# Converting float64 weights beside a recurrence: scaled high words moved from PSUM to SBUF, level products on two PSUM buffers

## The chip, the cores and the metric

The kernel runs on one core of one Trainium2 chip. The metric is the device time of one execution in microseconds. A core has five engines that run at the same time and meet only through semaphores: TensorE (PE) for matmuls, VectorE (DVE), ScalarE (ACT) and GpSimd (POOL) for work on elements, and SyncE (SP), which here only issues transfers. SBUF is the working memory of 128 partitions. PSUM is the small memory that TensorE writes its products to.

## What is computed

Two blocks, one after the other. The first is a recurrence over 768 time steps for 4 x 8 heads of width 48; the second is a pair of matrix products with a gate between them, on 3072 rows of width 384 and a hidden width of 2048.

```python
def _attn_ref(r, k, v, w, u):
    ...
    for t in range(S):
        kt, vt, rt, wt = (k[:, :, t], v[:, :, t], r[:, :, t], w[:, :, t])
        cur = np.einsum('bhd,bhe->bhde', u[None] * kt, vt)
        y[:, :, t] = np.einsum('bhd,bhde->bhe', rt, state + cur)
        state = wt[:, :, :, None] * state + np.einsum('bhd,bhe->bhde', kt, vt)
    ...

def _moe_ref(x, w_in, w_out):
    h = x @ w_in
    sp = np.maximum(h, 0.0) + np.log1p(np.exp(-np.abs(h)))
    g = h * erf(sp)
    return (g @ w_out).astype(np.float32)
```

r, k, v, w and u arrive as float32. `w_in` and `w_out` arrive as float64, and the kernel turns them into float32 by arithmetic on their 32-bit words.

## The kernel before

**Steps.** The time axis is cut into 12 steps of one 128-token chunk for two of the four batches (`n_steps`). Steps 0 to 3 and step 4 (`DIRECT`) run `attend`; steps 5 to 11 run `attend_late`. While the attention of step s runs, TensorE also works on the matrix products of earlier steps: `hidden` (line 742, the product with `w_in`) of step s-1, and `project` (line 771, the product with `w_out`) of step s-3. These are generators that are cut into pieces, and a piece is pulled at each of eight places in a step (`place(0)` to `place(7)`). In steps 1 and 2 one piece of `hidden` is pulled at each place. Piece number i of `hidden` reads columns 2i and 2i+1 of `w_in_sb`.

**Levels.** `attend` treats a chunk as a tree. For each level 1 to 6 it takes a PSUM buffer from `products`, writes 32 small products of r and k into it (`level_products`, line 444, 64 records in the profile), multiplies r and k by decays on VectorE (`scale`, line 260), and takes the products out of PSUM into `own` (line 661 for level 1, `copy_predicated` on line 456 for levels 2 to 5, two ScalarE copies on line 463 for level 6). The products of the next level read the r and k that line 260 has just scaled. After the six levels come the transposes of k (line 673), their copy `kT` (line 677), the products for the state (line 530), the new state on VectorE and GpSimd (lines 682, 701 to 706), and the products with the state (line 504), after which `xT`, the input of `hidden`, is copied out of PSUM (lines 511 to 514) and completed by small transfers (line 518).

The decays of the next step (`prepare`, line 312) are made on GpSimd, in products of 512, 256, 128, 64, 32 and 16 elements, between the levels.

**Weight conversion.** `convert` works on 16 blocks of 128 x 768 weights, blocks 0 to 7 for `w_in` and 8 to 15 for `w_out`. Each block takes five steps:

- `load` (line 196, SP) brings the 64-bit words into one of three buffers `words`;
- `scale` runs twice on ScalarE: line 209 multiplies the high words by a power of two into `base`, line 211 the low words into `rest` (two buffers);
- `shift` (line 217, VectorE) shifts the bits of `base` left by three;
- `join` (line 225, VectorE) takes the sign bit from `words`, puts it to the shifted bits and writes the block's place in `w_in_sb` or `w_out_sb`;
- and at the end of `join` GpSimd adds `rest` to that place (line 229). Only then may TensorE read the block.

The table `CONVERT` says by hand at which place of which step each of these is issued: `j` is a shift followed by a join, `h` a shift alone, `o` a join alone, `l` a load, `s` the two scalings. Blocks 0 and 1 are converted in step 0, blocks 2 to 7 in step 1, 8 to 13 in step 2, 14 and 15 in step 3. The order of each engine's instructions is the order of the program.

**PSUM.** Per partition, `y` takes 4 KB, the pool of `hidden` and `project` two buffers of 2 KB, and the two buffers `pp0` and `pp1` of `products` 4 KB each. `base` is the buffer `pp1`. So from the first scaling to the last join the levels use `pp0` alone (the flag `converting`), and `base` has one buffer: line 209 of a block can start only when line 225 of the block before it has read `pp1`. In step 1 the products for the state take `pp1`.

```python
n = 0 if turns["converting"] else turns["next"]
...
base = ps_p.tile([P, 2, NP * C], FP32, name="pp1")[:, :, :DM]
...
nc.scalar.mul(out=base, in_=high.bitcast(FP32), mul=2.0**-112)
...
nc.vector.tensor_scalar(
    out=bits, in0=bits, scalar1=3, scalar2=None, op0=ALU.logical_shift_left
)
...
into = weights[i][0].bitcast(I32)
nc.vector.scalar_tensor_tensor(
    out=into, in0=words[:, :, :, 1], scalar=-(1 << 31), in1=bits,
    op0=ALU.bitwise_and, op1=ALU.bitwise_or,
)
nc.gpsimd.tensor_tensor(out=into, in0=into, in1=rest[:], op=ALU.add)
```

Of the kernel before, what the change touches and what calls it, by code (L numbers as in the profile page):

```python
# [11 lines left out]
FP32 = mybir.dt.float32  # L12
I32 = mybir.dt.int32
U32 = mybir.dt.uint32
AF = mybir.ActivationFunctionType
ALU = mybir.AluOpType

P = 128
EP = 64
HC = 64  # L20
NC = 2
# [39 lines left out]
def kernel(  # L61
# [14 lines left out]
    nc = tc.nc  # L76
    PSUM = bass.MemoryType.PSUM

    n_steps, _, _, JP, C = rkw.shape
    NH, D = v.shape[2:]  # L80
    NP = JP // NJ
    NE = NH // JP
    NB, n_pairs = out.shape[:2]
    _, NT, DM = w_out.shape
# [13 lines left out]
    wide = ctx.enter_context(tc.tile_pool(name="wide", bufs=4))  # L98
    outs = ctx.enter_context(tc.tile_pool(name="outs", bufs=2))
    dram = ctx.enter_context(tc.tile_pool(name="dram", bufs=2, space=bass.MemoryType.DRAM))  # L100
    ps_p = ctx.enter_context(tc.tile_pool(name="ps_p", bufs=1, space=PSUM))
# [21 lines left out]
    w_out_sb = const.tile([P, NT, DM], FP32, name="w_out_sb")  # L123
    y = ps_y.tile([P, NE, NJ, NP // 2, C], FP32, name="y")

    turns = {"next": 0, "converting": False}

    def products(shape, n=None):


        if n is not None:
            return ps_p.tile(shape, FP32, name=f"pp{n}")
        n = 0 if turns["converting"] else turns["next"]
        turns["next"] = 1 - n
        return ps_p.tile(shape, FP32, name=f"pp{n}")

# [30 lines left out]
    def near_log(s):  # L167
        return NEAR_LOG - (s == DIRECT)
# [13 lines left out]
    def convert(weights):  # L182

        held = {}

        def load(i):
            if i >= len(weights):
                return  # L190
            dst, src = weights[i]
            if src.dtype == FP32:
                nc.sync.dma_start(out=dst, in_=src)
                return
            words = wide.tile([P, 2, DM, 2], I32, name="words", bufs=3)
            nc.sync.dma_start(
                out=words[:].rearrange("p i n two -> p i (n two)"), in_=src.bitcast(I32)
            )
            held[i] = [words]

        def scale(i):
            if i in held:
                words = held[i][0]
                low, high = words[:, :, :, 0], words[:, :, :, 1]
                base = ps_p.tile([P, 2, NP * C], FP32, name="pp1")[:, :, :DM]
                rest = wide.tile([P, 2, DM], I32, name="rest", bufs=2)


                nc.scalar.mul(out=base, in_=high.bitcast(FP32), mul=2.0**-112)

                nc.scalar.mul(out=rest[:], in_=low.bitcast(U32), mul=2.0**-29)
                held[i] += [base.bitcast(I32), rest]

        def shift(i):
            if i in held:
                bits = held[i][1]
                nc.vector.tensor_scalar(  # L217
                    out=bits, in0=bits, scalar1=3, scalar2=None, op0=ALU.logical_shift_left
                )

        def join(i):
            if i in held:
                words, bits, rest = held.pop(i)
                into = weights[i][0].bitcast(I32)
                nc.vector.scalar_tensor_tensor(  # L225
                    out=into, in0=words[:, :, :, 1], scalar=-(1 << 31), in1=bits,
                    op0=ALU.bitwise_and, op1=ALU.bitwise_or,
                )
                nc.gpsimd.tensor_tensor(out=into, in0=into, in1=rest[:], op=ALU.add)  # L229

        stages = {"l": load, "s": scale, "h": shift, "o": join}
        done = dict.fromkeys(stages, 0)
        for _ in range(3):
            load(done["l"])
            done["l"] += 1
        while True:
            what = yield
            for stage in {"j": "ho"}.get(what, what):
                stages[stage](done[stage])
                done[stage] += 1  # L240
            if weights[0][1].dtype != FP32:
                turns["converting"] = 0 < done["s"] and done["o"] < len(weights)
                turns["next"] = 0

    def rows(e, n=D):
        return slice(e * EP, e * EP + n)
# [181 lines left out]
    def parts_of(s):  # L428

        c, i = divmod(s, SPC)  # L430
        in_t, vt = loaded[s]
        made, tots, tot = ready[s]
        ends = tot.rearrange("p (n h) -> p n h", h=NC)
        return c, in_t, vt, made, states[i][c % 2], states[i][1 - c % 2], ends
# [183 lines left out]
    def attend(s, xT, place, behind):  # L618

        c, in_t, vt, made, S, S_next, ends = parts_of(s)  # L620
        K = in_t[:, 1]
        RK = in_t[:, 0:2]


        following = prepare(s + 1) if s + 1 < n_steps else iter(())
        own = made if s >= DIRECT else att.tile([P, NH, HC], FP32, name="own")

        def keep_busy(*columns):
            zeros = states[1][0][:].rearrange("p n d -> p (n d)")
            for n in columns if not s else ():  # L630
                nc.tensor.matmul(
                    y[:].rearrange("p e j q t -> p (e j q t)")[:, :n], lhsT=ident[:],
                    rhs=zeros[:, :n], start=True, stop=True, skip_group_check=True,
                )

        def stay_warm(times=1, where=None):
            for _ in range(times):
                ps = where or ps_m.tile([P, NP * C], FP32, name="m")
                nc.tensor.matmul(
                    ps[:], lhsT=ident[:], rhs=ws[s][:, :NP], start=True, stop=True  # L640
                )

        if s == DIRECT:
            next(following)
        for level in range(near_log(s) + 1 if s == DIRECT else 1, LOG + 1):
            rk = made[:] if level == 1 else RK
            pp = products([P, NE, JP, HC])
            level_products(pp, rk, level)
            if level == LOG and s == DIRECT:
                spread_blocks(s + 1, pp)  # L650
            scale(s, level)
            keep_busy(DM, DM // 2)
            if level == 1 and s == 1:
                stay_warm()
            if s == 1 and level == 2:
                behind(None)
            got = pp[:].rearrange("p e n t -> p (e n) t")
            if level == 1:
                if not s:
                    nc.vector.tensor_copy(out=first[:], in_=mask_sb[:, 0, :])  # L660
                nc.vector.tensor_mul(
                    own[:], got, first[:, None, :].to_broadcast([P, NH, HC])
                )
            else:
                take_level(own, pp, level)
            if level > 1 and (s, level) != (DIRECT, LOG - 1):
                next(following, None)
            place(level - 1)

        from_own(s, own, 1)  # L670
        ps = products([P, JP, P])
        for n in range(JP):
            nc.tensor.transpose(ps[:, n, :], K[:, n, :], ident[:])  # L673
        if not s:
            stay_warm()
        kT = att.tile([P, NH, D], FP32, name="kT", bufs=1)
        nc.scalar.copy(
            kT[:].rearrange("p (e n) d -> p e n d", e=NE),
            ps[:].rearrange("p n (e d) -> p e n d", e=NE)[..., :D],
        )  # L680
        if c:
            nc.gpsimd.tensor_mul(
                faded[0][:], S[:], ends[:, :, 0:1].to_broadcast([P, JP, D])
            )
        next(following, None)
        place(LOG)


        if s:

            ps = products([P, NC, JP, HC], 1 if s == 1 else None)
            ps = [ps[:, h] for h in range(NC)]
        else:
            ps = [ps_m.tile([P, JP, HC], FP32, name="m") for h in range(NC)]
        state_part(s, kT, ps)
        from_own(s, own, 0)
        if not s:
            stay_warm(1, products([P, NP * C]))
        for e in range(NE):
            if c:  # L700
                nc.vector.tensor_add(middle[rows(e)], faded[0][rows(e)], ps[0][rows(e), :, :D])
            else:
                nc.vector.tensor_copy(middle[rows(e)], ps[0][rows(e), :, :D])
        nc.gpsimd.tensor_mul(faded[1][:], middle[:], ends[:, :, 1:2].to_broadcast([P, JP, D]))
        for e in range(NE):
            nc.vector.tensor_add(S_next[rows(e)], faded[1][rows(e)], ps[1][rows(e), :, :D])
        for _ in following:
            pass
        place(LOG + 1)
        through_state(s, xT)  # L710
        behind()
# [135 lines left out]
    with tc.manual_schedule(  # L847
# [20 lines left out]
        for s in range(n_steps):  # L868
# [34 lines left out]
            def behind(n=0):  # L903
                if n is not None:
                    convert_at(LOG + 2)
                    return
                for what in BEHIND_SCALING:
                    conversion.send(what)
# [6 lines left out]
        s = n_steps - 1  # L915
# [105 lines left out]
```

## Time and profile before

| | |
|---|---|
| time, median of 3 runs | 616.99 us (616.94 to 617.49) |
| span of the profiled execution, first to last instruction | 614.9 us |
| granted TensorE clock | 1.000 |
| matrix products, line 742 / line 771 | 257.3 / 252.1 us |
| conversion on ScalarE: line 209 / line 211, 16 each | 0.888 / 0.912 us each (medians) |
| conversion on VectorE: line 217 / line 225, 16 each | 0.966 / 0.95 us each (medians) |
| conversion on GpSimd: line 229, 16 | 1.81 us at the least, up to 2.72 us |
| conversion, from the first to the last instruction | 25.6 to 120.0 us |

The profile gives no time of its own for the profiled execution beside its span; the median of the timed runs is 2.1 us longer than the span. Times in the profile count from the first instruction. "PEld" is the weight load of TensorE, which runs beside its products. A bracket at the end of a line of the timeline says how long the engine had been idle before the instruction and what released it.

### The profile page before, as it was taken

What the parts mean: (1) busy time and instruction counts of PE and PEld (TensorE: products, weight loads), DVE (VectorE), ACT (ScalarE), POOL (GpSimd) and SP (SyncE); (2) the same over time, 40 slices, a digit from 0 to 9 for tenths busy, and PEclk for the clock granted to TensorE, in tenths of its full rate; (3) what the DMA queues carried; (4) which work ended last, traced back from release to release, by engine and by line L of the source; (5) the groups of instructions that cost most, each with busy time, mean ns of one, the idle gap of its engine ahead of it and who ended that gap; (6) DMA issues with size and microseconds to landing.
All of it is one profiled execution on the core that took longest, in us unless ns stands there. A gap on an engine that the chain in (4) does not pass through costs nothing.

```text
span 614.9 us, 15592 instructions
## 1 busy us (share of the span) xinstructions
PE 602.1 (98%) x6858; PEld 445.9 (73%) x6858; DVE 409.3 (67%) x459; ACT 293.9 (48%) x374; POOL 293.3 (48%) x295
## 2 busy tenths in 40 slices
PE   7889999999999999999999999999999999999997
PEld 6668787678668668668668768768768768668654
DVE  5687696995995897897797797797797311110300
ACT  2548888544446724534534534534534444624600
POOL 4348184603497399299199299299296000000000
PEclk9999999999999999999999999999999999999999
DMA  8376471440353316307307306405303100000000
GB/s 325 117 281 203 184 258 58 164 149 8 136 157 78 101 34 190 112 29 206 101 30 197 109 31 181 126 31 156 117 28 79 25 26 0 9 26 1 0 27 26
DMA packets 51371, 63.27 MB, mean 103 GB/s; under 512 B 34920, under 2 KB 40296, under 8 KB 49896
## 3 DMA queue, kind: packets, MB, share of 16 engines
q1 hardware_dynamic: 50152, 61.68, 31.5%
q8 instruction: 54, 0.88, 0.6%
q10 hardware_dynamic: 1152, 0.59, 0.4%
q14 instruction: 13, 0.11, 0.1%
HBM read 52.39 MB, written 8.69 MB: 99 GB/s over the span
## 4 chain that ended last, share of the span: by engine, by line
PE 85%; DVE 6%; DMA 3%; POOL 2%; issue 2%; ACT 1%; SPq 0%; POOLq 0%; ACTq 0%; DVEq 0%
PE m L771 38%; PE m L742 37%; PE pp L444 4%; DMA w<-in_rkw 3%; PE y L478 2%; PE y L504 1%; PE pp L530 1%; DVE in L260 1%; POOL w_in_sb L229 1%; DVE w_in_sb L225 1%; POOL tot_sb L312 1%; PE pp L673 1%; DVE sums L364 1%; DVE pp L217 1%; DVE own L456 1%
## 5 line engine op out<-in xcount | busy, mean ns | idle before, releaser
L742 PE MATMUL m<-xT,w_in_sb 128*128 128x256 f32 x1152 | 257.3, 382 | 2.4 <-DVE w_in_sb L225 1.2
L771 PE MATMUL m<-w_out_sb,h 128*128 128x384 f32 x768 | 252.1, 488 | 0.0
L742 PEld LDWEIGHTS m<-xT,w_in_sb 128*128 128x128 f32 x1152 | 216.1, 190 | 34.8 <-issue 3.6
L771 PEld LDWEIGHTS m<-w_out_sb,h 128*128 128x128 f32 x768 | 144.6, 190 | 98.5
L751 ACT COPY h<-m 128x512 f32<-128x512 f32 x96 | 56.1, 584 | 130.5 <-PE m L742 130.4
L731 DVE TENSOR_TENSOR h<-h,sp 128x1024 f32<-128x1024 f32 x48 | 74.6, 1594 | 52.1 <-ACT sp L727 51.9
L260 DVE TENSOR_TENSOR in<-in,tot_sb 128x1024 f32<-128x1024 f32 (+1 forms) x60 | 84.4, 1414 | 30.6 <-PE pp L444 27.3
L378 POOL TENSOR_TENSOR words<-words,rest 128x528 f32<-128x528 f32 (+10 forms) x77 | 85.7, 1113 | 6.0
L374 POOL TENSOR_TENSOR rk<-words 128x528 f32<-128x528 f32 (+3 forms) x28 | 44.5, 1588 | 81.2 <-DVE sums L364 70.8
L780 ACT COPY o<-m 128x384 f32<-128x384 f32 x24 | 11.5, 480 | 110.3 <-PE m L771 110.3
L312 POOL TENSOR_TENSOR tot_sb<-tot_sb 128x256 f32<-128x256 f32 (+4 forms) x60 | 54.6, 911 | 4.5
L727 ACT ACTIVATE sp<-sp 128x2048 f32<-128x2048 f32 x24 | 45.9, 1911 | 0.3
L724 ACT ACTIVATE sp<-h 128x2048 f32<-128x2048 f32 x24 | 45.9, 1911 | 0.3
L444 PEld LDWEIGHTS pp<-in 48*64 48x64 f32 (+1 forms) x2368 | 33.8, 125 | 16.3 <-issue 8.5
L364 DVE TENSOR_REDUCE sums<-words 128x6 f32<-128x288 f32 (+8 forms) x66 | 29.2, 470 | 19.4 <-POOL words L374 19.2
L444 PE MATMUL pp<-in 48*64 48x64 f32 (+1 forms) x2368 | 38.3, 212 | 3.7 <-issue 1.6
L727 ACT ACT_TABLE_LOAD x24 | 30.8, 1283 | 15.9 <-issue 13.0
L374 POOL TENSOR_TENSOR words<-words 128x336 f32<-128x336 f32 (+6 forms) x49 | 35.1, 716 | 3.8
L364 DVE TENSOR_REDUCE sums<-rk 128x14 f32<-128x672 f32 (+9 forms) x54 | 34.8, 704 | 0.2
L724 ACT ACT_TABLE_LOAD x24 | 30.8, 1283 | 4.9 <-issue 4.5
L378 DVE TENSOR_TENSOR words<-words,rest 128x576 f32<-128x576 f32 (+8 forms) x34 | 27.9, 820 | 1.2
L229 POOL TENSOR_TENSOR w_out_sb<-w_out_sb,rest 128x768 int32<-128x768 int32 x8 | 17.8, 2222 | 17.8 <-DVE w_out_sb L225 17.7
(80 smaller groups left out, 438.0 us busy)
## 6 DMA issues: line engine op xcount, KB each, us to landing
in<-in_rkw SPq DMA_DIRECT2D x11, 1024.0 KB, 5.6
words<-in_moe_w_in SPq DMA_DIRECT2D x8, 768.0 KB, 4.5
words<-in_moe_w_out SPq DMA_DIRECT2D x8, 768.0 KB, 4.3
words<-in_rk_rows SPq DMA_DIRECT2D x8, 768.0 KB, 6.8
w<-in_rkw SPq DMA_DIRECT2D x11, 512.0 KB, 8.4
v<-in_v SPq DMA_DIRECT2D x12, 384.0 KB, 6.9
out<-o SPq DMA_DIRECT2D x24, 192.0 KB, 1.9
rest<-in_w_rows SPq DMA_DIRECT2D x8, 384.0 KB, 7.3
```

Of the source, the lines that this page charges most:

```text
L260: nc.vector.tensor_mul(halves, halves, view(tots[level - 1], 0, [[1, n], [2, nb], [0, half]]))
L312: nc.gpsimd.tensor_mul(new, pair[:, :, 0], pair[:, :, 1])
L364: nc.vector.tensor_reduce(out=view(sums[:], n, [[near * (NEAR + 1), NEAR // near], [NEAR + 1, near - n]]), in_=terms[n], axis=mybir.AxisLi ...
L374: engine.tensor_mul(terms[n], r[:, :, n:], k[:, :, : near - n])
L378: engine.tensor_mul(k[:, :, :m], k[:, :, :m], w[:, :, n : n + m])
L444: nc.tensor.matmul(pp[s0 : s0 + m, e, n, :m], lhsT=rk[rows(e), 1, n, s0 : s0 + m], rhs=rk[rows(e), 0, n, t0 : t0 + m], start=True, stop=True,)
L724: nc.scalar.activation(held[0][:], h[:], AF.Softplus)
L727: nc.scalar.activation(held[0][:], held[0][:], AF.Erf)
L731: nc.vector.tensor_mul(h[:, part], h[:, part], held[0][:, part])
L742: nc.tensor.matmul(ps[:, ff, :], lhsT=w_in_sb[:, g * FG + f + ff, kk * P : (kk + 1) * P], rhs=xT[:, kk, :], start=kk == 0, stop=kk == KT - 1,)
L751: nc.scalar.copy(h[:, f : f + FT, :], ps[:])
L771: nc.tensor.matmul(ps[j][:], lhsT=gs[g][:, f, j * C : (j + 1) * C], rhs=w_out_sb[:, g * FG + f, :], start=g + f == 0, stop=g == NG - 1 and ...
```

## The change

Three things change. `base` becomes a tile in SBUF with two buffers, and the shift writes its result straight into the block's place in `w_in_sb` or `w_out_sb`, so that the join reads it from there and works in place. With `pp1` free, `products` alternates between `pp0` and `pp1` throughout, and the flag `converting` and the fixed choice in step 1 go. The new tile takes 2 x 3 KB per partition of SBUF, and the program is built with `dynamic_dma_scratch_size=1024` in place of the default.

```diff
-    turns = {"next": 0, "converting": False}
+    turns = {"next": 0}
...
-        n = 0 if turns["converting"] else turns["next"]
+        n = turns["next"]
...
-                base = ps_p.tile([P, 2, NP * C], FP32, name="pp1")[:, :, :DM]
+                base = wide.tile([P, 2, DM], FP32, name="base", bufs=2)
...
-                nc.scalar.mul(out=base, in_=high.bitcast(FP32), mul=2.0**-112)
+                nc.scalar.mul(out=base[:], in_=high.bitcast(FP32), mul=2.0**-112)
...
-                held[i] += [base.bitcast(I32), rest]
+                held[i] += [base[:].bitcast(I32), rest]
...
-                    out=bits, in0=bits, scalar1=3, scalar2=None, op0=ALU.logical_shift_left
+                    out=weights[i][0].bitcast(I32), in0=bits, scalar1=3, scalar2=None, op0=ALU.logical_shift_left
...
-                words, bits, rest = held.pop(i)
+                words, _, rest = held.pop(i)
                 into = weights[i][0].bitcast(I32)
                 nc.vector.scalar_tensor_tensor(
-                    out=into, in0=words[:, :, :, 1], scalar=-(1 << 31), in1=bits,
+                    out=into, in0=words[:, :, :, 1], scalar=-(1 << 31), in1=into,
...
-            if weights[0][1].dtype != FP32:
-                turns["converting"] = 0 < done["s"] and done["o"] < len(weights)
-                turns["next"] = 0
...
-            ps = products([P, NC, JP, HC], 1 if s == 1 else None)
+            ps = products([P, NC, JP, HC])
...
-    nc = bacc.Bacc("TRN2", target_bir_lowering=False, num_devices=1)
+    nc = bacc.Bacc("TRN2", target_bir_lowering=False, num_devices=1, dynamic_dma_scratch_size=1024)
```

## The prediction

> **What bounds the kernel now.** First the busy times of the engines, then busy times by stretch, to see where TensorE is not full.
>
> ```profile
> PE 602.1 (98%) x6858; PEld 445.9 (73%) x6858; DVE 409.3 (67%) x459; ACT 293.9 (48%) x374; POOL 293.3 (48%) x295
> ```
>
> ```profile
> 34.00:58.00 24.00, 22.52 (x404) 17.96 (x408) 21.87 (x24) 15.83 (x25) 16.89 (x12) 1.00 0.79 273
> ```
>
> The columns of the second are the stretch, its length, the busy time of PE, PEld, DVE, ACT and POOL with their instructions, the clock and the transfers. TensorE is the bound; after 120 us nothing of the conversion runs. Whatever the change brings or costs is idle time of TensorE in steps 0 to 3, and it stays to the end, because afterwards TensorE runs almost without a gap (from 127 us on it is busy for 483.2 of 487.9). But from 34 to 58 us (step 1) VectorE is busy for 21.87 of 24 us, nearly as full as TensorE: a level costs TensorE 1.09 us on line 444 and 2.79 us on line 742, together 3.88, and VectorE 3.6 to 3.8 (from one line 260 to the next). Next the timeline of the conversion.
>
> ```profile
> 42.52 1.16 PE L444 MATMUL pp<-in 48*64 48x64 f32 x64 [0.78 <-DVE own L456]
> ...
> 47.76 1.22 DVE L260 TENSOR_TENSOR in<-in,tot_sb 128x1024 f32<-128x1024 f32 x1
> ...
> 47.98 2.67 POOL L229 TENSOR_TENSOR w_in_sb<-w_in_sb,rest 128x768 int32<-128x768 int32 x1 [0.94 <-DVE w_in_sb L225]
> ...
> 49.50 0.97 DVE L217 TENSOR_SCALAR pp<-pp 128x768 int32<-128x768 int32 x1
> ...
> 50.50 0.95 DVE L225 SCALAR_TENSOR_TENSOR w_in_sb<-words,pp 128x768 int32<-128x768 int32 x1
> 50.62 1.04 POOL L312 TENSOR_TENSOR tot_sb<-w 128x512 f32<-128x512 f32 x1
> ...
> 55.04 2.46 PEld L742 LDWEIGHTS m<-xT,w_in_sb 128*128 128x128 f32 x12 [0.24 <-POOL w_in_sb L229]
> ```
>
> Line 444 waited 0.78 us at 42.52 for line 456 to empty the only buffer (0.17 more at 76.12): all that two buffers can return. At 55.04 line 742 waited for GpSimd's line 229, so piece i of `hidden` starts as soon as block i is converted: the conversion is itself on the edge of the critical path. And the shift at 49.50 ran at its full rate in the middle of line 229 (47.98 to 50.65). Its operands are in PSUM. Other instructions of VectorE don't get past GpSimd so easily:
>
> ```profile
> 9.90 1.26 POOL L312 TENSOR_TENSOR tot_sb<-tot_sb 128x128 f32<-128x128 f32 x1
> 10.83 0.39 DVE L660 CAST first<-mask_sb 128x64 f32<-128x64 int32 x1
> ...
> 71.80 1.83 POOL L229 TENSOR_TENSOR w_out_sb<-w_out_sb,rest 128x768 int32<-128x768 int32 x1 [6.71 <-DVE w_out_sb L225]
> 73.23 1.49 DVE L260 TENSOR_TENSOR in<-in,tot_sb 128x1024 f32<-128x1024 f32 x1 [1.57 <-PE pp L444]
> ...
> 117.56 2.41 POOL L229 TENSOR_TENSOR w_out_sb<-w_out_sb,rest 128x768 int32<-128x768 int32 x1
> 118.34 2.25 DVE L378 TENSOR_TENSOR words<-words,rest 128x576 f32<-128x576 f32 x1
> ```
>
> Line 378 needs 0.75 us for this shape and took 2.25, line 260 needs 1.22 and took 1.49: each ended as if it had begun 0.14 us before the recorded end of line 229. The other way, the 2.67 of line 229 at 47.98 is 1.83 after line 260 let go, 0.14 before its end at 48.98. I use this rule everywhere: who comes second waits for the whole instruction of the other, then runs its full time; of two, the one that waits already goes next. (One case breaks the second half: at 111.08 a line 312 stood back for two of line 731.)
>
> [...] the shift from PSUM passed, and the cast at 10.83 (one input, SBUF to SBUF) ended 0.19 us after the GpSimd instruction let go at 11.02. [...] line 285, 256 elements, 0.289 us[...]. [...] here 0.888 us (line 209) against 0.912 (line 211).
>
> **The change, part by part.**
> *Scaling (line 209) to SBUF.* 16 times 0.024 us on ScalarE: nothing, hidden beside VectorE. Its waits for line 225 (10.5 us in all) go, but in steps 1 and 2 VectorE, not ScalarE, comes last. What is late next on ScalarE is line 211, which needs line 229 of two blocks before; by the times below its data are there before the join wants them.
> *Shift (line 217) in SBUF.* Lines 281 and 285 put the fixed part at 0.155 us and the double rate at 0.52 ns per element: 0.155 + 768 x 0.52 = 0.555 us in place of 0.966 (estimate). Bounds: 0.966 if no double rate. [...]
> *Join (line 225).* Same 0.95 us, but its second input is now in SBUF[...].
> *Two buffers for the levels.* The 0.78 and 0.17 us.
> *The build option.* No transfer is issued on GpSimd's queue: nothing.
>
> Step 1 by the rule. VectorE starts 0.09 us before the end of an independent predecessor, 0.03 after one that it needs; GpSimd 0.14 after VectorE; TensorE 0.05 after its releaser. Until 41.1 all stays (`xT` at 34.55 sets TensorE). Line 229 of block 2 runs 41.25 to 43.08. TensorE now starts level 3 at 41.74, but piece 2 needs block 2: 43.13, before 43.61, gain 0.48. Shift 3, ready at 42.28, waits until 42.94 and ends 43.50; join 3 ends 44.48, line 260 45.61 (each 0.26 late); line 229 of block 3, behind line 260, ends 47.30, piece 3 starts 47.35 (gain 0.14). Shift 4, ready 46.15, waits for that until 47.16, ends 47.72 (before 46.85); join 48.70; line 260 49.83; block 4 at 51.52, piece 4 at 51.57 (before 51.37). Shift 5, ready 50.37, waits until 51.38, ends 51.94. Now line 312 (512 elements, 1.04) has waited and goes first, to 52.84; join 5 52.70 to 53.65; line 312 (256, 0.62) to 54.13; line 260 53.99 to 55.21 (before 52.74), block 5 at 56.90 and piece 5 at 56.95 (before 55.04): 1.91 late. Again: shift 6 ends 57.32, join 6 58.39 behind a line 312, line 260 59.62, shift 7 60.14. There join 7 and line 229 of block 6 come within 0.01 us of each other; block 6 is ready at 62.81 or 62.01, so piece 6 starts 3.51 or 2.71 late (before 59.35). Then ScalarE, no longer held by its softplus (it ended at 65.32, line 504 at 65.50), returns 0.16: 3.35 or 2.55; I take 2.95.
>
> Step 2, in the old times. `w_out` isn't needed yet, so only line 260 can stop TensorE. Level 3 starts 0.17 earlier. Shift 10 waits to 80.51, shift 11 to 84.73, join 11 behind line 312 to 86.44, line 260 of level 5 to 88.00: level 6 at 88.05 (before 87.75). Line 260 of level 6 ends 92.41 (before 90.03), the transposes start 0.64 late. Then joins, line 229 twice, line 731 twice and line 682 take turns: line 682 ends at 100.15 (before 97.13), line 701 at 101.30, line 504 starts at 101.35 in place of 100.02: 1.33 late. Behind it stands TensorE's whole queue. Step 3: block 15 is ready at 120.1, before line 771 wants it at 121.08; nothing.
>
> Sum: 2.95 + 1.33 = 4.3 us on the span of 614.9, so 619.2; the median lies 2.1 above the span, and that part stays: 616.99 + 4.3 = 621.3.
>
> **The rivals.** *No double rate*: the shift keeps 0.97 us and passes GpSimd, only the joins meet it. By the same walk join 5 and line 312 meet at 50.6, piece 5 starts 0.74 late and piece 6 1.0 late, of which ScalarE returns 0.15 and step 2 0.17: +0.7, 617.7. For it: no tensor_scalar from SBUF is in the trace. Against: the cast and the copy. *No meeting* (not slower): in steps 1 and 2, shift and join get through beside line 229 although their operands are in SBUF. Then 0.48 + 0.17 us are gained: 616.3. It decides if a shift beside line 229 takes no more than 0.6 us. Against it stand the three cases above. *The same, and the gap of 1.00 us at 67.93* (TensorE waits for `xT`) closes as well: 1.65, 615.3. Against: that gap hangs on the softplus and the transfer of `xT`, which the change doesn't touch. *Worse turns*: [...] step 2 loses as much as step 1, 2 us more: 623.3.
>
> **How the numbers follow.** Main case 0.74 with its own range 619.5 to 623 (one turn of 0.8 us won or lost, the shift 0.1 us off); worse turns 0.05; no double rate 0.08; no meeting 0.06; with the gap 0.07. A measurement can tell 0.2% (1.2 us) from no change. Slower is 0.74 + 0.05 = 0.79, the same 0.08 + 0.06 = 0.14, faster 0.07. The range leaves out the last three, 0.21, and reaches from 618.4 (a third of the cost, if most turns fall as at 111.08) to 624.0 (worse turns, and 0.7 for one more).
>
> **What would show it.** Line 217 at 0.55 us where GpSimd is idle (block 0, at 26.5) and 1.2 to 1.7 us where line 229 runs (blocks 3 to 6); some joins above 0.95; the level 5 instance of line 260 in step 1 ending 2 to 3 us later; line 742 waiting 1 to 2.5 us for line 229 at pieces 5 and 6; no wait of line 444 for line 456. Wrong would be: shifts of 0.55 us in the midst of line 229, or 0.97 everywhere.

## The result, and the profile after

The changed kernel takes 622.62 us (median of 4 runs, 622.08 to 624.16) beside 617.24 us for the kernel before (4 runs, 616.94 to 617.64): a ratio of 1.0090, 95% interval 1.0074 to 1.0106. It is slower, by 5.4 us. The profiled run took 622.43 us, with a span of 620.6 (before 614.9). From line 241 on the lines of the changed kernel carry numbers lower by three: 257 is the old 260, 309 the old 312, 441 the old 444, 739 the old 742, 501 the old 504, 768 the old 771. Below, "the multiply" is line 260/257, "the add" is GpSimd's line 229.

The busy times of the engines on the page, and the same stretch of step 1 as was shown of before (stretch, its length, PE, PEld, DVE, ACT, POOL, clock, transfers):

```profile
PE 602.8 (97%) x6858; PEld 445.7 (72%) x6858; DVE 415.2 (67%) x459; ACT 293.6 (47%) x374; POOL 298.3 (48%) x295
```

```profile
34.00:58.00 24.00, 21.04 (x386) 16.71 (x387) 22.13 (x20) 14.96 (x24) 16.37 (x9) 1.00 0.73 254
```

TensorE has the same work (602.8 us beside 602.1) and 5.7 us more span, so 5 us more idle. VectorE was to be relieved: a shift costs 0.41 us less in SBUF. Yet it is busy for 5.9 us more in all, and in step 1 for 22.13 us in place of 21.87. In the records the time in which an instruction is held up counts as busy: the shift that takes 0.55 us with GpSimd idle is recorded for up to 1.60 us in the timeline of the changed kernel:

```profile
41.94 1.32 DVE L217 TENSOR_SCALAR w_in_sb<-base 128x768 int32<-128x768 int32 x1
...
45.91 1.58 DVE L217 TENSOR_SCALAR w_in_sb<-base 128x768 int32<-128x768 int32 x1
...
48.62 2.69 POOL L229 TENSOR_TENSOR w_in_sb<-w_in_sb,rest 128x768 int32<-128x768 int32 x1 [1.56 <-DVE w_in_sb L225]
...
50.14 1.60 DVE L217 TENSOR_SCALAR w_in_sb<-base 128x768 int32<-128x768 int32 x1
51.27 1.36 POOL L309 TENSOR_TENSOR tot_sb<-w 128x512 f32<-128x512 f32 x1
...
51.77 1.68 DVE L225 SCALAR_TENSOR_TENSOR w_in_sb<-words,w_in_sb 128x768 int32<-128x768 int32 x1
...
53.37 1.63 DVE L257 TENSOR_TENSOR in<-in,tot_sb 128x1024 f32<-128x1024 f32 x1
53.88 2.79 POOL L229 TENSOR_TENSOR w_in_sb<-w_in_sb,rest 128x768 int32<-128x768 int32 x1
...
56.72 2.86 PE L739 MATMUL m<-xT,w_in_sb 128*128 128x256 f32 x12 [0.91 <-POOL w_in_sb L229]
...
59.94 4.39 POOL L229 TENSOR_TENSOR w_in_sb<-w_in_sb,rest 128x768 int32<-128x768 int32 x2
...
62.62 0.70 PE L739 MATMUL m<-xT,w_in_sb 128*128 128x256 f32 x2 [1.42 <-POOL w_in_sb L229]
```

Read it downwards. The add of block 4 starts at 48.62. The shift at 50.14, which in PSUM ran beside it in 0.97 us, now ends at 51.74, 0.43 us after the recorded end of the add. GpSimd's line 309 comes next, the join behind the shift waits for that one (1.68 in place of 0.95), the multiply waits for the next (1.63 in place of 1.23), and the add of block 5, recorded from 53.88, waits in its turn (2.79 in place of 1.81). Piece 5 of `hidden` starts at 56.72 in place of 55.04, piece 6 at 62.62 in place of 59.35. The opening says that the engines meet only through semaphores; here VectorE and GpSimd hold each other up without one, too. The profile's summary of waits has no entry in which VectorE waits for line 229, though the shift at 50.14 took 1.05 us longer than with GpSimd idle. All the shifts of the changed kernel, shortest, median and longest, in ns:

```profile
L217 DVE TENSOR_SCALAR w_in_sb<-base x8: 559/1124/1599, 26.4 to 59.3; 128x768 int32<-128x768 int32 x8
L217 DVE TENSOR_SCALAR w_out_sb<-base x8: 550/778/1575, 73.0 to 118.1; 128x768 int32<-128x768 int32 x8
```

With GpSimd idle a shift takes 0.55 us; beside the add up to 1.6. The summary of waits has TensorE on the add itself (first the kernel before, then the changed one, two lines):

```profile
PEld m L742 <- POOL w_in_sb L229: 0.2, 1, 0.2
```

```profile
PEld m L739 <- POOL w_in_sb L229: 4.0, 5, 1.7
...
PE m L739 <- POOL w_in_sb L229: 3.2, 5, 1.4
```

The columns are us in total, times and the longest. Lastly a piece of the difference that has nothing to do with this waiting. At 440.6 us, long after the conversion, TensorE stops among the 64 small matmuls of line 501 (32 with the state `s`, then 32 with `middle`):

```profile
440.05 0.51 PE L501 MATMUL y<-in,s 48*48 48x64 f32 x23
441.74 0.36 PE L501 MATMUL y<-in,s 48*48 48x64 f32 x9 [1.18 <-issue]
```

"issue" says that nothing which the profile shows was late. In the kernel before, the same list runs through (30 of the 32 records with `s` stand in one row, and the next row follows without a gap):

```profile
435.44 0.86 PE L504 MATMUL y<-in,s 48*48 48x64 f32 x30
```

### The profile page after: what moved, and what is told of

The parts are those of the page before. It is cut to its first block, busy times and chain, and to the rows that moved or that the text cites. A ratio compares the mean times of both kernels' runs of the same rounds, so it can differ in the third digit from the quotient of the medians.

```text
span 620.6 us, 15584 instructions
## 1 busy us (share of the span) xinstructions
PE 602.8 (97%) x6858; PEld 445.7 (72%) x6858; DVE 415.2 (67%) x459; ACT 293.6 (47%) x374; POOL 298.3 (48%) x295
## 4 chain that ended last, share of the span: by engine, by line
PE 82%; DVE 7%; POOL 5%; issue 2%; DMA 1%; ACT 1%; SPq 0%; DVEq 0%; POOLq 0%; ACTq 0%
PE m L768 38%; PE m L739 35%; PE pp L441 4%; DVE in L257 2%; POOL tot_sb L309 2%; PE y L475 2%; PE y L501 2%; POOL w_out_sb L229 1%; PE pp L527 1%; POOL w_in_sb L229 1%; DMA in<-in_rkw 1%; DVE own L453 1%; DMA xT<-y 1%; DVE sums L361 1%; DVE words L375 1%
## 5 line engine op out<-in xcount | busy, mean ns | idle before, releaser
L728 DVE TENSOR_TENSOR h<-h,sp 128x1024 f32<-128x1024 f32 x48 | 77.0, 1644 | 51.6 <-ACT sp L724 51.4
L229 POOL TENSOR_TENSOR w_out_sb<-w_out_sb,rest 128x768 int32<-128x768 int32 x8 | 19.1, 2394 | 17.0 <-DVE w_out_sb L225 13.1
L375 DVE TENSOR_TENSOR words<-words,rest 128x576 f32<-128x576 f32 (+8 forms) x34 | 26.4, 776 | 1.2
```

The lines of the kernel that those rows point to most:

```text
L375: engine.tensor_mul(k[:, :, :m], k[:, :, :m], w[:, :, n : n + m])
L728: nc.vector.tensor_mul(h[:, part], h[:, part], held[0][:, part])
```

## Experiments

Theory: shift and join now have both sides in SBUF, they and GpSimd's instructions wait for each other, and this waiting costs more than the shift gains; the second buffer helps. The late gap comes from the number of TensorE's instructions ahead of it. Rivals: the shift's speed or the join alone is the cost; the second buffer makes it; the late gap is a late effect of the conversion.

The table takes each run's trace apart at one place. *To step 2* is the time from the first product of `hidden` in step 1 to the first product of `project` in step 2 (67.11 us before); *rest* is from there to the end of TensorE's last product (509.83 us before). Both are differences to before; the first holds the conversion, the second almost none of it.

| run | median us | ratio to before (95%) | to step 2 | rest |
|---|---|---|---|---|
| the change | 622.62 | 1.0090 (1.0074–1.0106) | +4.61 | +1.35 |
| e1, change without the add | 616.78 | 0.9992 (0.9982–1.0002) | −1.45 | +1.67 |
| e2, before without the add | 618.80 | 1.0025 (1.0017–1.0033) | +0.28 | +1.57 |
| e3, change, shift at single rate | 620.01 | 1.0042 (1.0028–1.0057) | +1.44 | +1.61 |
| e4, before, join in SBUF | 621.51 | 1.0071 (1.0051–1.0091) | +4.44 | +0.39 |
| e5, change, 22 warm-up multiplies | 621.53 | 1.0063 (1.0046–1.0081) | +4.61 | +0.50 |
| e6, before, 18 warm-up multiplies | 618.28 | 1.0008 (0.9999–1.0016) | −0.02 | +1.60 |
| e7, change with one buffer | 626.34 | 1.0131 (1.0107–1.0154) | +6.98 | +2.83 |
| e8, e4 with 22 warm-up multiplies | 621.79 | 1.0063 (1.0041–1.0086) | +3.14 | +0.24 |
| e9, change, add in halves | 623.50 | 1.0088 (1.0065–1.0112) | +4.28 | +1.97 |
| e10, before, add in halves | 617.90 | 0.9999 (0.9988–1.0011) | +0.49 | +0.20 |
| e11, e3 with the add in halves | 620.43 | 1.0037 (1.0025–1.0049) | +2.04 | +1.69 |

The kernel before had medians of 617.24, 617.40, 617.65 and 617.62 us in the four groups (change; e1 to e4; e5 to e8; e9 to e11). In *rest* two classes stand apart: 0.2 to 0.5, and 1.35 and more. Those of the second all have a gap of 1.1 to 1.5 us in the list of line 504/501 near 436 to 446 us, those of the first don't. What is left, 0.2 to 0.5 us, is mostly another gap in such a list, at 250 to 259 us, which was 0.94 us in the one profiled run of before and 1.0 to 1.4 in the others.

### Without the add (e1, e2)

```diff
-                nc.gpsimd.tensor_tensor(out=into, in0=into, in1=rest[:], op=ALU.add)
```

Both leave out the addition of the low words to the weights.

> The changed kernel without line 229: the low words of the weights are not added, all else stays. GpSimd then has only the decays (line 309) between the levels. Theory [...]: shifts fall to 0.56 us except where line 309 runs, TensorE waits for nothing of the conversion, and the kernel becomes faster than the one before, about 616.0 us (5.4 lost are back, and 0.78 + 0.17 + 0.24 us of waits of the kernel before are gone too). Rival (the cost is in the work on SBUF itself, or in the two buffers for the levels): line 229 was only running beside it, so about 621 to 622.6 us.

> The kernel before without line 229, as the counterpart of the run without it after the change: the low words are not added. Both theories: shifts and joins read PSUM and met nobody, so only 0.24 us (piece 5 waited for line 229) and a part of 0.17 us come back: about 616.9 us. If it fell by a microsecond or more, line 229 would cost something in itself, and the other run could not be read as it stands.

The change without its add costs nothing: 616.78 us, and to step 2 it is 1.45 us faster than before and 6.06 faster than the full change. It lies 0.8 us above the 616.0 expected; its profile has the late gap, with 1.12 us. The shifts of this kernel, where block 5 and 6 are converted:

```profile
49.30 0.55 DVE L217 TENSOR_SCALAR w_in_sb<-base 128x768 int32<-128x768 int32 x1
...
52.51 0.55 DVE L217 TENSOR_SCALAR w_in_sb<-base 128x768 int32<-128x768 int32 x1
53.08 0.96 DVE L225 SCALAR_TENSOR_TENSOR w_in_sb<-words,w_in_sb 128x768 int32<-128x768 int32 x1
```

1.60 us have become 0.55. So it is the meeting with the add, not the new shift or join as such. Taking the add away also takes away TensorE's wait for it, so e1 alone doesn't say how much is this waiting; e2 is there for that. e2 was a miss in size: 618.80 where 616.9 was expected, above before, though an instruction less was asked of GpSimd per block. Most of it, 1.57 us, lies in the rest, with a late gap of 1.19. The 0.28 us up to step 2 come from a meeting that the add had kept away: GpSimd, free early, now begins line 311 (the old 312) just ahead of the multiply.

```profile
44.36 1.04 POOL L311 TENSOR_TENSOR tot_sb<-w 128x512 f32<-128x512 f32 x1 [12.80 <-DMA w<-in_rkw]
44.43 2.04 DVE L259 TENSOR_TENSOR in<-in,tot_sb 128x1024 f32<-128x1024 f32 x1
```

The multiply waits for 0.8 us and TensorE for 0.48 after it. So without the add the two conversions differ by 0.28 + 1.45 = 1.73 us to step 2, in favour of the changed one; with it by 4.61 against it. The meetings with the add have turned the sign.

### The shift at single rate (e3)

```diff
-                base = wide.tile([P, 2, DM], FP32, name="base", bufs=2)
+                base = wide.tile([P, 3, 264], FP32, name="base", bufs=2)[:, :, :256]
```

The rows are kept apart by 8 words, with the scaling's and the shift's views cut to match. With this gap all 16 shifts took 0.93 to 1.00 us, beside GpSimd or not, so the double rate is off; why a gap does that is not shown by a run here.

> The changed kernel with the scaled high words in rows of 256 that have a gap of 8 words between them, 3 rows to a block[...]; the rest is the same. Theory: the shift then [...] takes 0.97 us everywhere, also beside line 229, and only the joins still meet GpSimd: 617.7 us (the rival 'no double rate' of the prediction), so a shift that is slower by 0.4 us makes the kernel 5 us faster. Rival (the joins carry the cost): still 621 us or more, and joins of 1.7 us. If the shift still takes 0.56 us where GpSimd is idle, the gap did not do what it should.

The profile of e3 around the add of block 4 (there line 234; the shift is 221, the join 230, the multiply 262):

```profile
50.05 2.67 POOL L234 TENSOR_TENSOR w_in_sb<-w_in_sb,rest 128x768 int32<-128x768 int32 x1 [0.96 <-DVE w_in_sb L230]
...
51.57 0.93 DVE L221 TENSOR_SCALAR w_in_sb<-base 128x768 int32<-128x768 int32 x1
52.53 1.00 DVE L230 SCALAR_TENSOR_TENSOR w_in_sb<-words,w_in_sb 128x768 int32<-128x768 int32 x1
52.69 1.75 POOL L314 TENSOR_TENSOR tot_sb<-w 128x512 f32<-128x512 f32 x1
...
53.46 2.06 DVE L262 TENSOR_TENSOR in<-in,tot_sb 128x1024 f32<-128x1024 f32 x1
```

The slower shift, SBUF to SBUF as in the change, runs through in the middle of the add in 0.93 us, and the kernel is 2.6 us faster than the change for it: of the 4.61 us up to step 2, 1.44 are left. So it is not the place of the operands alone that makes the shift wait: the one that takes 0.55 us with GpSimd idle needed 1.60 beside the add, the one of 0.93 us did not wait. Joins and multiplies still meet GpSimd (the multiply at 53.46 took 2.06 us in place of 1.21, the join at 57.02 1.56 in place of 1.00), and these 1.44 us, with the 1.61 of the rest (a late gap of 1.44 in it), give 620.01 in place of the 617.7 expected.

### The join in SBUF alone (e4, e8)

```diff
-                    out=bits, in0=bits, scalar1=3, scalar2=None, op0=ALU.logical_shift_left
+                    out=weights[i][0].bitcast(I32), in0=bits, scalar1=3, scalar2=None, op0=ALU.logical_shift_left
...
-                    out=into, in0=words[:, :, :, 1], scalar=-(1 << 31), in1=bits,
+                    out=into, in0=words[:, :, :, 1], scalar=-(1 << 31), in1=into,
```

`base` and the shift's input stay in PSUM. e8 differs from e4 in its warm-up multiplies alone (as e5 below).

> The kernel before, with one part of the change: the shift still reads PSUM, but writes into the weights' place, and the join reads it from there (two inputs in SBUF). Base stays in PSUM, the levels stay on one buffer. Theory: shifts stay at 0.97 us and pass line 229; the join meets line 312 once in step 1, piece 5 starts 0.74 and piece 6 1.0 us later, 0.15 come back: about 618.1 us. Rival (the joins carry the cost): 621 us or more.

> The kernel before with the shift's output in the weights' place (the shift still reads PSUM), as in the run of that before, and with 22 warm-up multiplies instead of 20 (4 of them narrow). That run had a TensorE gap of 1.16 us at 51.3 us in which nothing visible was late, and it came out at 621.5. If that gap depends on the program's layout, it is gone or elsewhere here, and the join's part alone is seen: 618.1 to 619.5 us. If the gap belongs to the edit: 621.5.

Both were dearer than expected. e4 had a second gap of the layout's kind, in the small matmuls of level 5; in e8, four TensorE records further on, it is gone:

```profile
50.20 1.14 PE L444 MATMUL pp<-in 48*64 48x64 f32 x58
...
52.50 0.34 PE L444 MATMUL pp<-in 48*64 48x64 f32 x6 [1.16 <-issue]
```

```profile
50.45 1.16 PE L444 MATMUL pp<-in 48*64 48x64 f32 x64
```

Of 4.44 us to step 2, 3.14 remained. Of these some 1.2 arise up to line 504 of step 2, from joins that wait for GpSimd, as expected. The other 1.9 us had not been thought of; the profile of e8 shows them at the end of step 2:

```profile
102.70 1.12 DVE L706 TENSOR_TENSOR s<-faded,pp 48x384 f32<-48x384 f32 x2 [1.01 <-POOL faded L704]
...
103.96 1.16 PE L444 MATMUL pp<-rk 48*64 48x64 f32 x64 [1.57 <-DVE s L706]
```

The level products of step 3 want the buffer that still holds the products for the state, and their reader, line 706, hangs on GpSimd (lines 682 and 704), which is behind with its adds. In the kernel before, line 706 had ended at 100.43, just ahead of line 444 at 100.57: the wait was 0.14 us from appearing. The medians of e4 and e8 don't differ, because three of e4's and four of e8's six runs had a mean granted clock of 0.997 or less, and took 621.55 to 623.86 and 621.40 to 623.44 us; of the runs above that, e4's are at 620.23, 620.25 and 621.47 us, e8's at 619.81 and 620.32.

### One buffer for the levels (e7)

```diff
-        n = turns["next"]
+        n = 0 if turns["converting"] else turns["next"]
```

with the flag `converting` set as before.

> The changed kernel with the level products on one PSUM buffer while the conversion runs, as in the kernel before; the scaled words stay in SBUF. This takes the change's second half away alone. If the second buffer brings next to nothing, because the level's multiply on VectorE rather than the buffer is what each level waits for: 622.6 us, within 0.5 either way. If it hides a cost of the first half (each level's matmuls then have to wait for the multiply of the level before, which now meets GpSimd): 624 or more.

626.34 us, and 2.37 us more than the change up to step 2. Not all of that is the buffer: in this profile the granted clock was 0.50 from 107.29 to 110.71 us, and the list of small products just before the first product of `project` falls into it.

```profile
106.86 1.67 PE L444 MATMUL pp<-rk 48*64 48x64 f32 x64 [1.57 <-DVE s L706]
```

From the start of this list to that product it is 1.61 us here and 1.10 in e8 at full clock. So 0.51 of the 2.37 us belong to the clock, and the second buffer is worth about 1.9 us up to step 2. Most of this is the wait of 1.57 us for line 706, which the change doesn't have. Another 1.1 us of the clock lies in the first 16 product records of line 771 (6.52 us in place of 5.43), in the rest. The two runs without such a drop, at 624.84 and 624.88, are 2.2 us above the median of the change and 2.4 above its profiled run. So the change's first half alone costs about 6.5 us up to step 2, and its second half takes 1.9 of them back.

### The late gap (e5, e6)

```diff
-        for _ in range(20):
-            nc.tensor.matmul(warm[:], lhsT=ident[:], rhs=ident[:], start=True, stop=True)
+        for n in [P] * 18 + [16] * 4:
+            nc.tensor.matmul(warm[:, :n], lhsT=ident[:], rhs=ident[:, :n], start=True, stop=True)
```

This is e5; e6 is the kernel before with `range(18)`.

> The changed kernel, with 22 warm-up multiplies instead of 20 at its start (18 of full width and 4 of 16 columns, so that they take no more time). The weight conversion is untouched. If the TensorE gap of 1.18 us at 440.6 us, which the kernel before does not have, depends only on how many TensorE instructions stand ahead of that place, it moves off the dense small matmuls and is gone: 621.4 us, 1.2 under the changed kernel, with the conversion's cost of 4.7 us unchanged. If the gap is an effect of the conversion, or of something else that comes late for it, it stays: 622.6.

> The kernel before, with 18 warm-up multiplies instead of 20, and nothing else changed. If the late gap depends only on the number of TensorE instructions ahead of it, this kernel now gets one of about 1.2 us near 437 us: 618.5 us. If the gap comes from the changed conversion, none appears here: 617.3.

The list of line 501 in e5, and of line 504 in e6:

```profile
440.88 0.82 PE L501 MATMUL y<-in,s 48*48 48x64 f32 x30
```

```profile
435.93 0.52 PE L504 MATMUL y<-in,s 48*48 48x64 f32 x24
437.69 0.33 PE L504 MATMUL y<-in,s 48*48 48x64 f32 x8 [1.25 <-issue]
```

Two multiplies more at the start and the gap of the change is gone, with the conversion's cost the same to the hundredth (+4.61); two fewer and the kernel before has it. It belongs to the position in TensorE's program, not to the conversion.

The traces show this position exactly. Number all of TensorE's records (weight loads, products and waits for semaphores) in the order of their starts: in each of the eight traces that have it, the late gap comes after 11,457 records. In all thirteen traces that place falls into this list. Where 21 to 27 of the list's products were out by then, TensorE stops for 1.1 to 1.5 us; where it was 14 to 20, the next product comes within 0.2 us. The change moves the list because its TensorE program has six waits fewer (88 for 94), which is as many records as three products with their weight loads: 23 products are out where it was 20. e2 has eight waits fewer, and has the gap as well. So the gap came with the edit, but through the length of the program and not through the waiting between VectorE and GpSimd.

In the timed runs the steps are blurred: 1.1 us less in e5 than in the change, 0.6 more in e6 than before (interval −0.1 to +1.0).

### The add in halves (e9, e10, e11)

```diff
-                nc.gpsimd.tensor_tensor(out=into, in0=into, in1=rest[:], op=ALU.add)
+                for f in range(2):
+                    nc.gpsimd.tensor_tensor(out=into[:, f], in0=into[:, f], in1=rest[:, f], op=ALU.add)
```

> The changed kernel with GpSimd's add of each block (1.81 us alone) as two instructions of half the block, about 0.9 us each. If whoever comes second waits for one whole instruction of the other, VectorE's shift, join and multiply wait for a half at most: where the shifts of blocks 4 to 6 lasted 1.55 to 1.60 us, at most 1.2 (0.56 of its own and one half, less 0.14), and pieces 5 and 6 come sooner; worked out from the 3.5 us lost there, about half comes back: 621.0 us. Rival: the two keep taking turns, so that each half now waits for one VectorE instruction and the add of a block ends later than before (over 2.8 us for the two): 622.6 or above. A TensorE gap of about 1.2 us in line 501's list may come or go with the layout.

> The kernel before with the same edit. Here only the level's multiply and the add meet (the shift and the join have a PSUM side), so a half as much wait is worth little: 617.0 us, within 0.5 apart from a late gap of about 1.2 us that the layout may bring. Rival: the add's second half comes behind a multiply and the weights come later: 618 or above without such a gap.

> The changed kernel with the shift at single rate (which passes GpSimd) and the add in halves: only joins and multiplies meet the add, and for a half at most. The single-rate shift alone came out at 620.0, with a late gap of the layout in it. If waits go by whole instructions, some 0.8 us of the 1.4 lost there up to step 2's first projection come back: 619.2 us, or 618.0 where the layout brings no late gap. Rival: turns take it back: 620.0.

The profile of e9 in step 1 (the add is line 230 there, two instructions to a row):

```profile
45.94 3.14 POOL L230 TENSOR_TENSOR w_in_sb<-w_in_sb,rest 128x384 int32<-128x384 int32 x2 [0.97 <-ACT rest L211]
...
47.47 0.75 DVE L217 TENSOR_SCALAR w_in_sb<-base 128x768 int32<-128x768 int32 x1
...
48.25 1.64 DVE L225 SCALAR_TENSOR_TENSOR w_in_sb<-words,w_in_sb 128x768 int32<-128x768 int32 x1
```

The shift waits for half an add only, 0.75 in place of 1.58. But then it is the second half's turn, and the join waits for that, 1.64 in place of 0.96: together 2.39 us for 2.54. The two halves take 3.14 us for one add of 2.67 (block 3). This is the rival, and the time went its way: 1.0088 beside 1.0090 for the change, and 622.68 us in the one run at full clock. The profiled run had the clock at 0.50 from 57.62 to 61.03 us, so that piece 5 took 4.54 us in place of 2.86; piece 6 was not held up by that, as it began at 63.48, 0.06 us after the first half of its add. Of the 0.86 us by which piece 5 came sooner than in the change, 0.33 were left at step 2. In e10 and e11 halving brings nothing either: up to step 2 it costs 0.49 us beside the kernel before and 0.6 beside e3.

No version here beats the kernel before: the nearest that does the whole work is e10, at 0.9999.

## Why the prediction was right

621.3 us were predicted and 622.62 measured. The mechanism holds, and the walk through step 1 can be compared term by term, once it is known that the profiled run of the change had everything before it 0.22 us earlier (`hidden` starts at 34.33 in place of 34.55).

| | predicted | measured + 0.22 |
|---|---|---|
| shift with GpSimd idle | 0.555 us long | 0.55 to 0.56 us long |
| shifts 3, 4, 5, 6, 7 end | 43.50, 47.72, 51.94, 57.32, 60.14 | 43.48, 47.71, 51.96, 57.31, 60.12 |
| joins 3, 4, 5, 6 end | 44.48, 48.70, 53.65, 58.39 | 44.48, 48.70, 53.67, 58.38 |
| level 5's multiply ends | 55.21 | 55.22 |
| piece 5 starts | 56.95 (1.91 late) | 56.94 |
| piece 6 starts | 3.51 or 2.71 late | 3.49 late |

- *Shift and meeting.* Right. That a shift at double rate and a join with both inputs in SBUF would wait for GpSimd, and a shift at single rate would not, was the author's assumption; the kernel before showed waiting only for other instructions (the cast at 10.83, lines 260 and 378). The runs bear it out: the new shift took up to 1.60 us and the new join up to 1.68 where GpSimd was at work, and e3's shift 0.93 us in the midst of the add. The double rate was the author's estimate from two instructions of 256 elements, a multiply of 0.426 us (line 281) and a copy of 0.289 us (line 285), and the 0.55 us agree with its 0.555.
- *The tossed turn.* Join 7 and the add of block 6 were within 0.01 us; both are recorded at 59.94, and the adverse turn came: the piece starts 3.49 late, and what remains after ScalarE's return is 3.46 (the wait for `xT` that ended at 68.93 ends at 72.17), where 2.95 was taken between 3.35 and 2.55. This is half a microsecond of the error.
- *Step 2.* 1.33 us predicted at line 504. There it waits for line 698 until 104.54 in place of 100.02, which is 4.74 later from the start of `hidden`, so 1.28 beside the 3.46; 1.15 are left at the first product of `project`. *Step 3*: nothing, and from 106 to 120 us TensorE of the changed kernel is busy for 14.00 of 14.
- *Two buffers.* "All that two buffers can return" was put at 0.78 + 0.17 us. For the waits that the kernel before has, this is right. As the value of the second buffer it was too small: e7 shows about 1.9, since the first half makes new waits for the one buffer. The sum didn't suffer, because the walk was made with two buffers.
- *Scaling and option.* The scaling into SBUF took 0.925 us (median) in place of 0.888, more than the 0.024 allowed for, and stayed hidden. The build option was not tried by itself; e1, which has it, is no slower than the kernel before.
- *What was missing* is the late gap of 1.18 us. The sum of the trace: 4.61 to step 2, 1.35 in the rest, less 0.22 for the earlier start, is 5.74, the 5.7 by which the spans differ. Against 4.3 predicted this is +0.5 for the turn, −0.2 in step 2, +1.35 and −0.2. That the conversion's part alone came out at 4.4 for 4.3 is partly luck, because the first two and the last of these nearly cancel.

Of the rivals, "no meeting" and "the gap at 67.93 closes" fell with the first shift at 1.6 us; that gap is still 0.86. "No double rate" was made in e3: its pieces 5 and 6 come 0.64 and 1.02 late, against 0.74 and 1.0 in the text, but the price of the whole, 0.7, was too low. ScalarE returned nothing (the next wait for `xT`, at 67.93 to 68.93 before, ends 1.09 late), and 0.35 more came in step 2, which had been credited with a gain. "Worse turns", 623.3 (in step 2 the add of block 9 ahead of the multiply), is nearer to the measured time than the main case; the trace tells them apart. In step 2 the multiply began at 80.35 and the add of block 9 at 80.49, the order of the main case, and step 2 cost 1.15 us.

## What to carry to other kernels

Before a result is moved from PSUM to SBUF on VectorE to run at double rate, look at what GpSimd does at that moment: here the shift of 0.97 us from PSUM ran beside GpSimd's add, and the one of 0.55 us in SBUF, which saves 0.41 us, waited up to 1.0 us, and what followed on both engines came later with it (piece 6 of `hidden` by 3.49 us). Cutting GpSimd's add into halves only moved the waiting (shift and join together 2.39 us for 2.54, e9); what eased it was a shift that did not wait, although it was slower by 0.4 us (e3, 2.6 us less than the change). And a second buffer's worth is not read from the waits that exist (0.78 and 0.17 us), but from those that the rest of the change makes (about 1.9 us, e7).

## What the runs showed of the hardware

- TensorE can stop for a microsecond and more inside a list of small matmuls with nothing late that the profile shows (1.18 us in the change). The thirteen traces hold 43 stops of over 0.3 us for which the profile names no releaser, and all 43 come after 449, 705, 1985, 7617 or 11,457 of TensorE's records, weight loads and waits counted. Each of these numbers is 193 more than a multiple of 256. Whether TensorE stops at such a place depends in part on how far the list has run (the late gap above), and in part on what stays open: 1985 falls 58 products into level 5's list in e1, e2 and e4, and only e4 stops. Transfers of 16 KB on the instruction queue lie beside the late gap (439.4 and 442.9 us in the change), but before has such transfers at 433.4 and 437.1 with no gap. What makes TensorE stop there was not shown. Two warm-up multiplies more removed a gap of 1.18 us (e5), and two fewer in the kernel before brought one of 1.25 us (e6), 0.2% of the time in both.
- The granted clock halves for some 3.4 us in a part of the executions (four times in the profiles of e3, e7 and e9, each time for 3.41 us). In e7's profile, after TensorE's gap of 1.57 us (stretch, length, busy times, clock, transfers):

```profile
106.00:107.00 1.00, 0.14 (x8) 0.17 (x12) 0.95 (x3) 0.70 (x3) 0.00 (x0) 1.00 0.00 0
107.00:108.00 1.00, 1.00 (x55) 1.00 (x56) 0.97 (x1) 0.00 (x0) 0.00 (x0) 0.65 0.10 26
108.00:109.00 1.00, 1.00 (x22) 0.84 (x16) 0.42 (x1) 0.38 (x1) 0.00 (x0) 0.50 0.23 58
```

  The drop lasts from 107.29 to 110.71 us, and full clock is back in the stretch from 111 us. TensorE had stood still from 105.29 to 106.86 us, and the clock fell 0.43 us after that. What sets off a drop was not shown. Most of the scatter goes with the drops: six of e1's 22 runs have a mean clock of 0.997 or less and took 617.93 to 619.99 us, the other 16 took 616.33 to 617.21. Such runs are 3 of 5 in e7, 4 of 6 in e8, 5 of 6 in e9, but 1 of 22 in e6 and none of 6 in e5, whose gaps are those of the change; a gap is not enough, then.
- Less work on one engine can make another wait longer (e2): the free GpSimd started its next instruction 0.07 us before VectorE's multiply, which then took 2.04 us in place of 1.22. This cost 0.28 us up to step 2; the larger part of the 1.4 us by which e2 is slower than before is the late gap.
- Time that VectorE spent waiting for GpSimd stands in these records as part of the instruction's duration (the shift: 0.55 us with GpSimd idle, up to 1.60 us beside the add). A mean per line hides it; the shortest and the longest (559 and 1599 ns) show it.
